# Attention and mixture-of-experts kernel: expert weights issued behind nearly all q, k and V loads, two more of them in the expert stage, scatters of skipped rows issued after their batch's gate

## Chip, cores, metric

The kernel runs on one core of one Trainium2 chip. The metric is device time in microseconds (us) of one execution, all executions judged by state (an execution over 1.5% above the fastest of its kernel counts as slow and is left out of the ratios). "Span" is the profiler's span of one execution; in these runs it is about 1.8 us shorter than the device time of the same execution.

## The reference

```python
# attention: 4 batches, 8 heads, 768 positions, head size 64; 8 global keys, 96 local keys
scores = scale * q @ k.T + bias            # bias: slope of the head times the distance
scores = where(is_global | is_local, scores, -1e9)
x = (softmax(scores) @ v)                  # as rows: x is [3072, 512]
# mixture of experts with early exit: 8 experts, hidden size 1024
do_compute = x @ w_skip > 0                # other rows leave as they are ("skipped rows")
e_idx = argmax(x @ w_gate);  gate_w = softmax(x @ w_gate)[e_idx]
out = x
out[do_compute] = x + gate_w * (relu(x @ w1[e_idx]) @ w2[e_idx])
```

## The kernel before

It works in three stages. Attention goes over 16 units (4 batches of 4 head pairs). The gate of a batch runs within the next batch's units; the last batch's gate stands alone. Then the expert stage: for each expert, gather its rows (two DMAs of 128 rows), multiply, and scatter the result `y` to `out`. Rows that skip the experts are scattered from SBUF, 24 DMAs of 128 rows.

Every load that casts float32 to bfloat16, every gather and every scatter is issued by GpSimd, in program order. One "half" is `w1` or `w2` of one expert: 2 MB read as float32, 1 MB written as bfloat16. There are 16.

```python
    def load_qk(n):                                  # 192 KB each
        nc.gpsimd.dma_start(out=kr[:, :, :], in_=k_r[...])
        nc.gpsimd.dma_start(out=qr[:, :, :], in_=q_r[...])
    def load_half(i, pool):                          # w1 (i even) or w2 (i odd) of expert i // 2
        ...
    EARLY = 5
    wq = list(range(2 * EARLY))                      # ten halves during attention
    halves = {1: 1, 2: 1, 3: 1, 4: 1, 5: 1, 6: 1, 7: 1, 8: 1, 9: 1, 10: 1}
    ...
    for n in range(NU):                              # units
        ...                                          # scores of n + 2, values of n, transposes of n + 4
        if m + 4 < NU:
            load_qk(m + 4)                           # m + 4 = n + 8: q, k of the last units go out at n = 7
        for kind in range(3):
            if extra:
                load_v(vb_, t)                       # 18 V loads, over after n = 5
        for _ in range(halves.get(n, 0)):
            load_half(wq.pop(0), wearly)
        ...                                          # gate and slot placement of batch b - 1
    ...
    def experts(group, first):
        rows, src, gate_ = slot_rows()
        for e in range(E):
            gather(e, src)                           # 2 DMAs
            if first and e % 2 == 1 and EARLY + e // 2 < E:
                load_half(2 * (EARLY + e // 2), wlate)
                load_half(2 * (EARLY + e // 2) + 1, wlate)
        xt = expert_in(0)
        for e in range(E):
            nxt = expert_in(e + 1) if e + 1 < E else None
            expert(e, xt, rows, gate_, group)        # ends in 2 y scatters; y has bufs=4
            if first:
                for t in range(3 * e, 3 * e + 3):
                    skip_out(t, group)               # scatter of skipped rows
            xt = nxt
```

The softmax here doesn't subtract the row's maximum and nothing guards it: scores larger than these inputs give would overflow.

Of the kernel before, what the change touches and what calls it, by code (L numbers as in the profile page):

```python
# [17 lines left out]
def kernel(  # L18
# [13 lines left out]
    nc = tc.nc  # L32
# [3 lines left out]
    T = S // 128  # L36
    N = B * S
    NT = N // 128
    DM = H * D
    HP = H // 2  # L40
    E, F = moe_w1.shape[0], moe_w1.shape[2]
# [13 lines left out]
    EARLY = 5  # L55
# [5 lines left out]
    wearly = ctx.enter_context(tc.tile_pool(name="wearly", bufs=1))  # L61
# [21 lines left out]
    def load_qk(n):  # L83
        b, hp = units[n]
        qr = raw_pool.tile([P, 2, R * D], BF16, tag="qr", name="qr")
        kr = raw_pool.tile([P, 2, R * D], BF16, tag="kr", name="kr")
        nc.gpsimd.dma_start(out=kr[:, :, :], in_=k_r[b, :, 2 * hp:2 * hp + 2, :])
        nc.gpsimd.dma_start(out=qr[:, :, :], in_=q_r[b, :, 2 * hp:2 * hp + 2, :])  # L88
        raws[n] = (qr, kr)
# [6 lines left out]
    def load_v(b, t):  # L96
        nc.gpsimd.dma_start(out=vbs[b][:, t, :, 0:D], in_=v_r[b, t])  # L97
# [3 lines left out]
    def load_half(i, pool):  # L101
        e = i // 2
        if i % 2 == 0:
            w1_sb[e] = pool.tile([128, DC, F], BF16, name=f"w1_{e}")
            nc.gpsimd.dma_start(out=w1_sb[e][:, :, :], in_=w1_r[e])
        else:
            w2_sb[e] = pool.tile([128, FC // 2, 2 * DM], BF16, name=f"w2_{e}")
            nc.gpsimd.dma_start(out=w2_sb[e][:, :, :], in_=w2_r[e])
# [30 lines left out]
    for h in range(H):  # L139
        nc.sync.dma_start(out=vg_f[h * KG:(h + 1) * KG, :, :],  # L140
                          in_=v[:, h, 0:KG, :].rearrange("b k d -> k b d"))
# [27 lines left out]
    for h in range(H):  # L169
        nc.scalar.activation(out=mask8[:, h, :, :],  # L170
                             in_=rel[:, :].unsqueeze(1).to_broadcast([128, 2, W]),
# [57 lines left out]
    skip_k = keep.tile([128, NT], I32)  # L229
# [3 lines left out]
    xbs = [keep.tile([128, T, DM], BF16, name=f"xb{b}") for b in range(B)]  # L233
# [30 lines left out]
    def keys_global(n):  # L264
        b, hp = units[n]
        nc.vector.tensor_tensor(
            out=kg[b % 2][:, hp, 2 * hp * KG:2 * (hp + 1) * KG].rearrange("p (h k) -> p h k", h=2),
            in0=kts[n][:, 0:KG].unsqueeze(1).to_broadcast([128, 2, KG]),
            in1=half_m[:, :].unsqueeze(2).to_broadcast([128, 2, KG]), op=ALU.mult)

    def global_scores(b):
        g_sb = att_pool.tile([128, S], BF16, tag="g_sb", name="g_sb")
        for u in range(2):
            gp = ps_ms.tile([128, R, P // 2], FP32, tag="ms", name="gp")
            for hp in range(HP):
                nc.tensor.matmul(out=gp[:, :, :], lhsT=kg[b % 2][:, hp, :],
                                 rhs=qts[b * HP + hp][:, :, u * (P // 2):(u + 1) * (P // 2)],
                                 start=(hp == 0), stop=(hp == HP - 1))
            nc.scalar.activation(
                out=g_sb[:, u * (S // 2):(u + 1) * (S // 2)].rearrange("a (p r) -> a p r", r=R),  # L280
                in_=gp[:, :, :].rearrange("a r p -> a p r"), func=ACT.Exp, bias=gbias[:, 0:1], scale=scale)
        nc.vector.tensor_tensor(out=g_sb[:, 0:128], in0=g_sb[:, 0:128], in1=m0g[:, :], op=ALU.mult)
        g_sbs[b] = g_sb
# [164 lines left out]
    def place(t0, nt, colid, pool, psum, tag):  # L448
        lo_i = pool.tile([128, nt], I32, tag="lo_i", name="lo_i")
        hi_i = pool.tile([128, nt], I32, tag="hi_i", name="hi_i")  # L450
        nc.vector.tensor_single_scalar(out=lo_i[:, :], in_=s_k[:, t0:t0 + nt], scalar=127,
                                       op=ALU.bitwise_and)
        nc.vector.tensor_single_scalar(out=hi_i[:, :], in_=s_k[:, t0:t0 + nt], scalar=7,
                                       op=ALU.arith_shift_right)
        ohc = pool.tile([128, nt, NCOL], BF16, tag="ohc", name="ohc")
        nc.vector.tensor_tensor(out=ohc[:, :, :],
                                in0=colid[:, :].unsqueeze(1).to_broadcast([128, nt, NCOL]),
                                in1=hi_i[:, :].unsqueeze(2).to_broadcast([128, nt, NCOL]),
                                op=ALU.is_equal)
        bv = pool.tile([128, nt, NV, NCOL], BF16, tag="bv", name="bv")  # L460
        nc.vector.tensor_tensor(
            out=bv[:, :, :, :],
            in0=ohc[:, :, :].unsqueeze(2).to_broadcast([128, nt, NV, NCOL]),
            in1=val_k[:, t0:t0 + nt, :].unsqueeze(3).to_broadcast([128, nt, NV, NCOL]), op=ALU.mult)
        oha = pool.tile([128, nt, 128], BF16, tag="oha", name="oha")
        nc.vector.tensor_tensor(out=oha[:, :, :],
                                in0=row128_i[:, :].unsqueeze(1).to_broadcast([128, nt, 128]),
                                in1=lo_i[:, :].unsqueeze(2).to_broadcast([128, nt, 128]),
                                op=ALU.is_equal)
        sp = psum.tile([128, NV, NCOL], FP32, tag=tag, name="slot_ps")  # L470
        for t in range(nt):
            nc.tensor.matmul(out=sp[:, :, :].rearrange("p a c -> p (a c)"), lhsT=oha[:, t, :],
                             rhs=bv[:, t, :, :].rearrange("p a c -> p (a c)"),
                             start=(t == 0), stop=(t == nt - 1))
        nc.vector.tensor_tensor(out=slots[:, :, :], in0=slots[:, :, :], in1=sp[:, :, :], op=ALU.add)




    extra = [("v", 1, t) for t in range(T)]  # L480
    wq = list(range(2 * EARLY))
    for b in (2, 3):
        extra += [("v", b, t) for t in range(T)]
    halves = {1: 1, 2: 1, 3: 1, 4: 1, 5: 1, 6: 1, 7: 1, 8: 1, 9: 1, 10: 1}
    for n in range(4):
        transposes(n, 1)
        transposes(n, 0)
# [7 lines left out]
    for n in range(NU):  # L495
        b, hp = units[n]
        if hp == 0:
            global_scores(b)
        m, j = n + 4, n + 2
        if j < NU:  # L500
            scores(j, 0)
        values(n, 0)
        if j < NU:
            scores(j, 1)
        if m < NU:
            transposes(m, 1)
            keys_global(m)
        if b > 0 and hp < 3:
            logits(b - 1, hp)
        if j < NU:  # L510
            scores(j, 2)
        values(n, 1)
        if m < NU:
            transposes(m, 0)
        if m + 4 < NU:
            load_qk(m + 4)
        if n in (0, 2, 4):
            make_v(1 + n // 2)
            load_vg(1 + n // 2)
        for kind in range(3):  # L520
            if extra:
                _, vb_, t = extra.pop(0)
                load_v(vb_, t)
        for _ in range(halves.get(n, 0)):
            load_half(wq.pop(0), wearly)
        if hp == HP - 1:
            x_out(b)
        if b > 0 and hp == 2:
            gate(b - 1)
        if b > 0 and hp == 3:  # L530
            gate_rest(b - 1)
            place((b - 1) * T, T, colid_i, gat_pool, ps_ms, "ms")
    for s in range(3):
        logits(B - 1, s, on_vector=(s == 1))
    gate(B - 1)
# [6 lines left out]
    wlate = ctx.enter_context(tc.tile_pool(name="wlate", bufs=1, reuse_waits="tile"))  # L542
# [21 lines left out]
    def gather(e, src):  # L564
        xg[e] = ffn.tile([128, 2, DM], BF16, tag="xg", name="xg", bufs=E)
        for c in range(2):
            nc.gpsimd.indirect_dma_start(  # L567
                out=xg[e][:, c, :], out_offset=None, in_=x_dram[:, :],
                in_offset=bass.IndirectOffsetOnAxis(ap=src[:, 2 * e + c:2 * e + c + 1], axis=0))

    def put(ins, group):
        tc.declare_no_dep(ins.ins, group=group, reason="each row is written once")
        tc.add_to_no_dep_group(group, ins.ins)

    def skip_out(t, group):
        put(nc.gpsimd.indirect_dma_start(  # L576
            out=out[:, :],
            out_offset=bass.IndirectOffsetOnAxis(ap=skip_k[:, t:t + 1], axis=0),
            in_=xbs[t // T][:, t % T, :], in_offset=None, bounds_check=N - 1, oob_is_err=False),
            group)  # L580

    def expert_in(e):
        xp = ps_x.tile([128, DC, CAP], BF16, tag="xp", name="xp")
# [35 lines left out]
    def experts(group, first):  # L619
        rows, src, gate_ = slot_rows()  # L620
        for e in range(E):
            gather(e, src)
            if first and e % 2 == 1 and EARLY + e // 2 < E:
                load_half(2 * (EARLY + e // 2), wlate)
                load_half(2 * (EARLY + e // 2) + 1, wlate)
        xt = expert_in(0)
        for e in range(E):
            nxt = expert_in(e + 1) if e + 1 < E else None
            expert(e, xt, rows, gate_, group)
            if first:  # L630
                for t in range(3 * e, 3 * e + 3):
                    skip_out(t, group)
            xt = nxt

    experts("first", True)
# [58 lines left out]
```

## Time and profile before

| | before |
|---|---|
| device time, median of the runs beside the kernel after | 242.93 us (242.35 to 243.9) |
| span of the profiled run | 242.2 us |
| last attention output | 123.2 us |
| first gather issued | 138.81 us |
| first y scatter issued, landed (after the first gather) | 34.4, 46.1 us |
| TensorE stall on y | 7.68 us |
| last expert matmul ends, end of span (after the first gather) | 80.5, 103.4 us |

Averages over the span say little here, as each stage has its own limit. In the profile PE is TensorE's matmul, PEld its weight load, DVE VectorE, ACT ScalarE and POOL GpSimd. These are the rows of the page that show the stages: one digit per fortieth of the span, about 6 us, in tenths busy; the clock row has the granted TensorE clock, in tenths of full speed.

```profile
PE   1579895995494847768544038699943999992000
DVE  7555896689826236837874611213003332213000
POOL 8776397253443620000000088271716777777710
PEclk9999998897569575559857556999995799998555
DMA  5999999999999999999630039999994355343310
```

The DMA engines are busy throughout attention and idle before the gathers. GpSimd does nothing from 91 to 138 us (eight zeros), while it is the last engine at work, after TensorE, at the end.

**Attention.** Two rows of TensorE's timeline (start, duration, instruction; in brackets the idle time before it and what ended it):

```profile
79.73 0.85 PE L251 MATMUL tr<-ident,kr 96*64 96x96 bf16 x16 [4.26 <-DMA kr<-in_k_dram]
89.22 0.85 PE L251 MATMUL tr<-ident,kr 96*64 96x96 bf16 x16 [3.53 <-DMA kr<-in_k_dram]
```

Units 9 and 10 wait for k. In the trace these two loads were issued at 62.66 and 74.64 and took 17.0 and 14.5 us to land, each right behind a weight half in the queue; the early k loads took about 7.5 us. The windows of the two units (columns: start and end; length; busy time and count of PE, PEld, DVE, ACT, POOL; granted clock; DMA share, which can pass 1 as the tool counts it and is not used here; GB/s) show the price of the wait in the clock as well, 0.62 and 0.68. In the 3.4 us behind each of the two waits it was 0.50:

```profile
76.30:84.60 8.30, 4.87 (x66) 3.75 (x67) 3.60 (x11) 3.01 (x6) 4.03 (x6) 0.62 1.55 192
84.60:94.10 9.50, 5.97 (x100) 4.91 (x98) 3.68 (x10) 4.28 (x6) 1.65 (x3) 0.68 1.15 210
```

**Experts.** GpSimd's timeline: L567 gathers, L105 and L108 weight halves, L614 y scatters, L576 skip scatters.

```profile
152.33 1.01 POOL L567 DMA_INDIRECT xg<-x_rows,src  x1 [0.30 <-issue]
157.31 1.01 POOL L567 DMA_INDIRECT xg<-x_rows,src  x1 [3.97 <-DMA w<-in_moe_w_dram]
...
160.83 0.82 POOL L105 DMA_DIRECT2D w<-in_moe_w_dram  x1
161.62 0.82 POOL L108 DMA_DIRECT2D w<-in_moe_w_dram  x1
164.36 1.02 POOL L567 DMA_INDIRECT xg<-x_rows,src  x1 [1.92 <-DMA w<-in_moe_w_dram]
169.40 1.01 POOL L567 DMA_INDIRECT xg<-x_rows,src  x1 [4.01 <-DMA w<-in_moe_w_dram]
...
173.21 1.03 POOL L614 DMA_INDIRECT out_dram<-y,rows  x1 [0.30 <-DMA xg<-x_rows,src]
174.54 1.00 POOL L614 DMA_INDIRECT out_dram<-y,rows  x1 [0.30 <-issue]
178.20 0.99 POOL L576 DMA_INDIRECT out_dram<-xb,skip_k  x1 [2.65 <-DMA w<-in_moe_w_dram]
183.14 1.00 POOL L576 DMA_INDIRECT out_dram<-xb,skip_k  x1 [3.94 <-DMA w<-in_moe_w_dram]
184.44 0.99 POOL L576 DMA_INDIRECT out_dram<-xb,skip_k  x1 [0.30 <-issue]
...
230.09 1.00 POOL L576 DMA_INDIRECT out_dram<-xb,skip_k  x1 [0.30 <-DMA out_dram<-xb,skip_k]
```

Two readings follow. First, count back eight DMA issues from each one that waited for `w`: it is always the half that had just landed (157.05, 164.10, 169.13, 177.94, 182.87; the waiting issue starts 0.26 to 0.27 us later). So every issue waits for the eighth before it. Second, from 183.14 to the end GpSimd issues one scatter every 1.3 us (1.0 busy, 0.3 between) without a pause.

The y scatter issued at 173.21 landed at 184.95, 2.1 us behind the last half. Until then VectorE had no free y buffer, and TensorE stalled in the middle of expert 3 (VectorE's and TensorE's timelines):

```profile
185.07 1.41 DVE L611 SCALAR_TENSOR_TENSOR y<-yps,gate,xg 128x512 f32<-128x512 f32 x2 [18.55 <-DMA out_dram<-y,rows]
```

```profile
185.87 3.57 PE L606 MATMUL yps<-w,ht 128*128 128x512 bf16 x8 [7.68 <-DVE y L611]
```

### The profile page before, as it was taken

The page shows a single profiled execution, that of the slowest core. Times are in us where ns is not written, and L with a number is a line of the kernel's source. Part 1 is how long each engine was busy: PE and PEld are TensorE (multiplying, and loading weights), DVE is VectorE, ACT ScalarE, POOL GpSimd, SP SyncE. Part 2 cuts the span into 40 slices and gives each one's busy share as a digit, 9 for nine tenths or more (in the row PEclk, how much of TensorE's full clock was granted, in tenths as well). Part 3 has the DMA queues.
Part 4 walks back from the last instruction along what each step waited for, and adds up shares of the span by engine and source line. Part 5 has one row for each costly group of instructions (what it writes and reads, how often), then busy time and mean ns, then how long its engine had stood idle before and what let it go on. Part 6 is the DMA issues. An engine that isn't in the chain of part 4 may idle for free. (4 is left out here: it accounts for less than half of the span.)

```text
span 242.2 us, 4714 instructions
## 1 busy us (share of the span) xinstructions
PE 155.8 (64%) x1877; PEld 110.8 (46%) x1877; DVE 109.1 (45%) x341; ACT 91.8 (38%) x144; POOL 111.0 (46%) x139
## 2 busy tenths in 40 slices
PE   1579895995494847768544038699943999992000
PEld 1455773774353635536544016377621766670000
DVE  7555896689826236837874611213003332213000
ACT  5865983992346433529303002133210222330000
POOL 8776397253443620000000088271716777777710
PEclk9999998897569575559857556999995799998555
DMA  5999999999999999999630039999994355343310
GB/s 79 151 170 194 156 134 189 240 195 185 209 227 209 187 210 209 211 226 237 118 133 0 1 87 177 249 213 237 191 263 132 95 153 153 104 133 110 113 36 0
DMA packets 50521, 38.25 MB, mean 158 GB/s; under 512 B 30276, under 2 KB 39492, under 8 KB 50496
## 3 DMA queue, kind: packets, MB, share of 16 engines
q0 software_dynamic: 45568, 34.62, 85.9%
q1 hardware_dynamic: 4928, 3.30, 5.4%
q8 instruction: 16, 0.26, 0.4%
q14 instruction: 9, 0.07, 0.1%
HBM read 54.68 MB, written 13.63 MB: 282 GB/s over the span
## 5 line engine op out<-in xcount | busy, mean ns | idle before, releaser
L567 POOL DMA_INDIRECT xg<-x_rows,src x16 | 15.7, 980 | 62.2 <-DVE gate L559 48.6
L602 ACT ACTIVATE ht<-hps 128x512 bf16<-128x512 f32 x32 | 19.1, 597 | 65.7 <-PE hps L599 65.7
L315 DVE TENSOR_TENSOR a<-a,mask 128x896 bf16<-128x896 bf16 (+1 forms) x48 | 28.2, 588 | 21.8 <-ACT a L301 11.7
L611 DVE SCALAR_TENSOR_TENSOR y<-yps,gate,xg 128x512 f32<-128x512 f32 x16 | 11.9, 750 | 54.8 <-PE yps L606 33.4
L606 PE MATMUL yps<-w,ht 128*128 128x512 bf16 x128 | 30.8, 395 | 7.7 <-DVE y L611 7.7
L301 ACT ACTIVATE a<-sc 128x896 bf16<-128x896 f32 x32 | 29.0, 923 | 11.2 <-PE sc L296 10.0
L599 PE MATMUL hps<-xt,w 128*128 128x256 bf16 x256 | 31.2, 283 | 0.0
L576 POOL DMA_INDIRECT out_dram<-xb,skip_k x24 | 24.1, 1004 | 13.3 <-DMA w<-in_moe_w_dram 6.6
L599 PEld LDWEIGHTS <-w 128*128 128x128 bf16 x256 | 25.9, 102 | 3.8
L97 POOL DMA_DIRECT2D vb<-in_v_dram x24 | 21.5, 906 | 11.3 <-DMA vb<-in_v_dram 4.0
L606 PEld LDWEIGHTS <-ht 128*128 128x128 bf16 x128 | 12.8, 100 | 22.2 <-issue 9.6
L296 PE MATMUL sc<-qt,kt 64*128 64x224 bf16 x192 | 20.3, 303 | 2.8 <-DVE qt L255 1.3
L333 PE MATMUL av<-vb,a 128*128 128x65 bf16 x192 | 20.7, 215 | 0.0
L251 PE MATMUL tr<-ident,kr 96*64 96x96 bf16 x256 | 11.4, 251 | 13.3 <-DMA kr<-in_k_dram 13.3
L340 PE MATMUL av<-vb,a 128*96 128x65 bf16 x160 | 19.7, 229 | 0.0
L88 POOL DMA_DIRECT2D qr<-in_q_dram x16 | 10.4, 650 | 19.2 <-DMA w<-in_moe_w_dram 11.7
L333 PEld LDWEIGHTS <-a 128*128 128x128 bf16 x192 | 18.6, 125 | 0.0
L346 DVE TENSOR_TENSOR xb<-av,rc 128x384 bf16<-128x384 f32 x32 | 17.8, 558 | 1.1
L614 POOL DMA_INDIRECT out_dram<-y,rows x16 | 15.9, 994 | 4.9 <-issue 3.7
L340 PEld LDWEIGHTS <-a 128*96 128x96 bf16 x160 | 17.1, 147 | 0.0
L251 PEld LDWEIGHTS <-kr 96*64 96x64 bf16 x256 | 8.8, 140 | 17.1 <-DMA kr<-in_k_dram 14.0
L259 ACT ACTIVATE kt<-tr 128x768 bf16<-128x768 bf16 x16 | 13.0, 810 | 8.5 <-PE tr L251 8.5
(117 smaller groups left out, 228.7 us busy)
## 6 DMA issues: line engine op xcount, KB each, us to landing
w<-in_moe_w_dram POOLq DMA_DIRECT2D x16, 1024.0 KB, 17.1
kr<-in_k_dram POOLq DMA_DIRECT2D x16, 192.0 KB, 7.8
qr<-in_q_dram POOLq DMA_DIRECT2D x16, 192.0 KB, 7.9
vb<-in_v_dram POOLq DMA_DIRECT2D x24, 128.0 KB, 10.2
x_rows<-xb SPq DMA_DIRECT2D x4, 768.0 KB, 9.3
out_dram<-xb,skip_k POOLq DMA_INDIRECT x24, 2.6
xg<-x_rows,src POOLq DMA_INDIRECT x16, 12.1
out_dram<-y,rows POOLq DMA_INDIRECT x16, 2.8
```

What stands on the lines that cost most here:

```text
L97: nc.gpsimd.dma_start(out=vbs[b][:, t, :, 0:D], in_=v_r[b, t])
L251: nc.tensor.transpose(out=ps[hh * D:(hh + 1) * D, r, :], in_=raw[:, hh, r * D:(r + 1) * D], identity=ident[0:P, 0:P])
L296: nc.tensor.matmul(out=sc[:, hh, kk, 0:R * wp].rearrange("a (r p) -> a r p", r=R), lhsT=kt[rows, t * 128:(t + 1) * 128], rhs=qt[rows, :, t ...
L301: nc.scalar.activation(out=a[:, :, :].rearrange("a h (k p r) -> a h k p r", k=2, r=R), in_=sc[:, :, :, 0:W].rearrange("a h k (r p) -> a h ...
L315: nc.vector.tensor_tensor(out=a[:, :, 0:wid], in0=a[:, :, 0:wid], in1=m[:, :, 0:wid], op=ALU.mult)
L333: nc.tensor.matmul(out=av[:, jj, hh, :], lhsT=a_sbs[n, t // 2][:, hh, (t % 2) * W:(t % 2) * W + 128], rhs=vb[:, t, h, :], start=False, sto ...
L340: nc.tensor.matmul(out=av[0:NL, jj, hh, :], lhsT=a_sbs[n, p // 2][:, hh, c:c + NL], rhs=vb[:, p, h, :], start=False, stop=(jj == 2 and hh ...
L346: nc.vector.tensor_tensor(out=xb[:, 3 * u:3 * u + 3, 2 * hp * D:(2 * hp + 2) * D].rearrange("p j (h d) -> p j h d", h=2), in0=av[:, :, :, ...
L576: put(nc.gpsimd.indirect_dma_start(out=out[:, :], out_offset=bass.IndirectOffsetOnAxis(ap=skip_k[:, t:t + 1], axis=0), in_=xbs[t // T][:, ...
L599: nc.tensor.matmul(out=hps[:, j, :], lhsT=w1_sb[e][:, dc, c2 * 256 + j:(c2 + 1) * 256:2], rhs=xt[:, dc, :], start=(dc == 0), stop=(dc == D ...
L602: nc.scalar.activation(out=ht[:, c2, :, :], in_=hps[:, :, :], func=ACT.Relu)
L606: nc.tensor.matmul(out=yps[:, :], lhsT=ht[:, f // 2, f % 2, c * 128:(c + 1) * 128], rhs=w2_sb[e][:, f // 2, (f % 2) * DM:(f % 2 + 1) * DM] ...
```

## The change

The intent: keep the weights from delaying q, k and V, and take the skip scatters off GpSimd's busiest stretch by issuing them where GpSimd is idle. It has three parts:

- A: the early halves start in unit 6 instead of unit 1. Unit 6's half still stands ahead of the last q and k loads, those of unit 7.
- B: 18 of the 24 skip scatters are issued before the gathers, two per unit once their batch's gate is done: those of batches 0 and 1 in the units of batches 2 and 3, those of batch 2 behind the last unit. The last batch's six stay with experts 1 to 3.
- C: only eight halves (experts 0 to 3) are loaded early; expert 4's two go into the expert stage, which now has eight halves instead of six.

```diff
-    halves = {1: 1, 2: 1, 3: 1, 4: 1, 5: 1, 6: 1, 7: 1, 8: 1, 9: 1, 10: 1}
+    skips = []
+    halves = {n: 1 for n in range(6, 14)}
 ...  (unit loop)
+        for _ in range(2):
+            if skips:
+                skip_out(skips.pop(0), "first")
         if b > 0 and hp == 3:
             gate_rest(b - 1)
             place((b - 1) * T, T, colid_i, gat_pool, ps_ms, "ms")
+            skips += range((b - 1) * T, b * T)
+    while skips:
+        skip_out(skips.pop(0), "first")
 ...  (experts)
             gather(e, src)
-            if first and e % 2 == 1 and EARLY + e // 2 < E:
-                load_half(2 * (EARLY + e // 2), wlate)
-                load_half(2 * (EARLY + e // 2) + 1, wlate)
+            if first and e % 2 == 1:
+                for i in range(2):
+                    load_half(2 * (E - 4) + e - 1 + i, wearly if e == 1 else wlate)
 ...
             if first:
-                for t in range(3 * e, 3 * e + 3):
-                    skip_out(t, group)
+                if e > 0 and e < 4:
+                    for t in range(NT - T + 2 * e - 2, NT - T + 2 * e):
+                        skip_out(t, group)
```

(The helpers `put` and `skip_out` only move up in the file.)

More of the change, by code (lines that the diff above doesn't have):

```diff
@@ L475, in place, with put, skip_out @@
         nc.vector.tensor_tensor(out=slots[:, :, :], in0=slots[:, :, :], in1=sp[:, :, :], op=ALU.add)
+    def put(ins, group):
+        tc.declare_no_dep(ins.ins, group=group, reason="each row is written once")
+        tc.add_to_no_dep_group(group, ins.ins)
+    def skip_out(t, group):
+        put(nc.gpsimd.indirect_dma_start(
+            out=out[:, :],
+            out_offset=bass.IndirectOffsetOnAxis(ap=skip_k[:, t:t + 1], axis=0),
+            in_=xbs[t // T][:, t % T, :], in_offset=None, bounds_check=N - 1, oob_is_err=False),
+            group)
     extra = [("v", 1, t) for t in range(T)]
     wq = list(range(2 * EARLY))
+    skips = []
     for b in (2, 3):
         extra += [("v", b, t) for t in range(T)]
-    halves = {1: 1, 2: 1, 3: 1, 4: 1, 5: 1, 6: 1, 7: 1, 8: 1, 9: 1, 10: 1}
+    halves = {n: 1 for n in range(6, 14)}
     for n in range(4):
@@ L569, in gather @@
                 in_offset=bass.IndirectOffsetOnAxis(ap=src[:, 2 * e + c:2 * e + c + 1], axis=0))
-    def put(ins, group):
-        tc.declare_no_dep(ins.ins, group=group, reason="each row is written once")
-        tc.add_to_no_dep_group(group, ins.ins)
-    def skip_out(t, group):
-        put(nc.gpsimd.indirect_dma_start(
-            out=out[:, :],
-            out_offset=bass.IndirectOffsetOnAxis(ap=skip_k[:, t:t + 1], axis=0),
-            in_=xbs[t // T][:, t % T, :], in_offset=None, bounds_check=N - 1, oob_is_err=False),
-            group)
     def expert_in(e):
```

## The prediction

> **What bounds the kernel now** (page, windows, timelines): three stages with different limits.
> 1. Attention, to 122.7 us. Units take about 4.2 us at full clock, set by VectorE and TensorE. In units 9 and 10 TensorE waits for a k load: 4.26 us (until 79.73) and 3.53 us (until 89.22). Those loads took 17.0 and 14.5 us to land, because 1 MB weight halves stood before them in the queue; early k loads take about 7.5. A half takes 4.9 to 5.3 us of DMA time.
> 2. Gate of the last batch: first gather at 138.81 us. The DMA row shows 0 here.
> 3. Experts. In GpSimd's timeline every DMA issue waits for the landing of the eighth before it, so six weight halves hold the gathers; the first y scatter issues at 173.21, landing at 184.95, behind the last half (182.87). TensorE stalls 7.68 us on y (four buffers), resumes at 185.87, ends at 219.3. GpSimd issues scatters unbroken, 1.3 us each, until 231; the chain of waits ends there. Last landing 232.7, then 9.5 us to the end, 242.2.
>
> **What the change does.**
> - Halves of experts 0 to 3 move to units 6 to 13, behind nearly all q, k loads: the two k stalls go, and cold clock with them. The Trainium skill, "TensorE: Matmul & The Clock Gate", Part 1, says about 3.4 us of idling halves the clock; this trace agrees (0.50 around both stalls). Units 9 and 10 took 8.3 and 9.5 us; I expect 4.3 each. Gain 8.9 us: first gather at about 130.
> - 18 of 24 skip scatters leave the expert stage: 18 x 1.3 = 23.4 us of GpSimd. They fit into gaps before the gathers. But GpSimd ends only about 11 us after TensorE, so at most 11 can be won.
> - Two more halves (expert 4) enter the expert stage: 2 x 5 = 10 us, in front of the first y scatter. By the eighth-before rule and queue order, expert 0's y lands about 56 us after the first gather instead of 46. TensorE's stall grows from 7.7 to about 18, and its end moves from 80.5 to about 91 us after the first gather. The Trainium skill, "DMA: Bandwidth & Descriptors", "Issuing engines are not separate DMA queues", says all DMAs share 16 engines; the trace agrees (that scatter lands 2.1 us after the last half).
>
> So the expert stage ends with TensorE, not GpSimd: last landing about 94.5, end about 104 us after the first gather; today 103.4. What freeing GpSimd gains, the longer y stall eats.
>
> **Sum.** 243.1 - 8.9 (k stalls, clock) - 11 (backlog) + 10.5 (y stall) + 0.5 = 234.2; I say 234.5 us, range 230.5 to 239. Chances: faster by over 2% 0.84, within 2% 0.14, slower 0.02.
>
> **What would show it.** No TensorE wait on k loads after the start; first gather near 130; DMA busy until about 100 us, idle before the gathers; VectorE's wait for y's scatter about 28 us, TensorE stalled about 18 within expert 3; no back-to-back scatters at the end, TensorE's last matmul within 4 us of the last landing.
>
> **What would make it wrong.** The y stall not growing (scatters overtaking weights, or halves faster than 5 us): about 225. The attention gain lost to other waits, or the clock at half after the gates: about 240. GpSimd, blocked on skip rows, holding a weight half so long that it meets the gathers: slower.

## The result, and the profile after

| | before | after |
|---|---|---|
| device time, median | 242.93 us | 235.87 us (235.46 to 236.07) |
| ratio, 95% interval | | 0.9703 (0.9669 to 0.9738) |
| span of the profiled run | 242.2 | 234.0 |
| units 9 and 10 | 8.3, 9.5 | 4.1, 4.2 |
| first gather issued | 138.81 | 129.33 |
| first y scatter issued, landed (after the first gather) | 34.4, 46.1 | 40.4, 58.2 |
| TensorE stall on y | 7.68 | 19.54 |
| last expert matmul ends, end of span (after the first gather) | 80.5, 103.4 | 91.7, 104.7 |

Times in us. A ratio is the mean time of one kernel's fast runs over that of the kernel before's fast runs of the same rounds, so it is not quite the ratio of the medians quoted.

The same rows of the page, after:

```profile
PE   1569995985769757695451179699800079999700
DVE  7554996498845888478838021130000061232300
POOL 8765596666572232641360775633436057333210
PEclk9999997699758985598575559999965569999975
DMA  5999999999999999999960299999999633311110
```

GpSimd now works through attention and thins out at the end. But TensorE has a hole of three slices (zeros), 170 to 187 us, in the middle of the expert stage; before, a smaller one stood there.

Units 9 and 10 in windows, to be set against the two of before: half as long, and the clock is 1.00.

```profile
76.40:80.50 4.10, 3.59 (x80) 2.83 (x79) 3.43 (x10) 3.96 (x7) 0.93 (x2) 1.00 1.12 210
80.50:84.70 4.20, 2.90 (x75) 2.41 (x69) 3.47 (x11) 2.99 (x5) 0.99 (x1) 1.00 1.19 238
```

GpSimd's timeline in the expert stage (L585 gathers, L621 y scatters, L482 skip scatters):

```profile
164.75 0.82 POOL L105 DMA_DIRECT2D w<-in_moe_w_dram  x1
165.54 0.84 POOL L108 DMA_DIRECT2D w<-in_moe_w_dram  x1
169.73 1.04 POOL L621 DMA_INDIRECT out_dram<-y,rows  x1 [3.35 <-DMA w<-in_moe_w_dram]
174.65 1.02 POOL L621 DMA_INDIRECT out_dram<-y,rows  x1 [3.87 <-DMA xg<-x_rows,src]
...
220.33 0.97 POOL L621 DMA_INDIRECT out_dram<-y,rows  x1 [4.25 <-DVE y L618]
222.06 0.97 POOL L621 DMA_INDIRECT out_dram<-y,rows  x1 [0.76 <-DVE cnt_i L650]
```

Expert 7's two halves now stand right ahead of the first y scatter, in the program and in the queue. At the end GpSimd waits for VectorE's y instead of running a backlog. VectorE and TensorE in the middle:

```profile
187.66 1.41 DVE L618 SCALAR_TENSOR_TENSOR y<-yps,gate,xg 128x512 f32<-128x512 f32 x2 [30.41 <-DMA out_dram<-y,rows]
```

```profile
188.47 3.40 PE L613 MATMUL yps<-w,ht 128*128 128x512 bf16 x8 [19.54 <-DVE y L618]
```

So the whole gain, 8.2 us of span, is in attention (the first gather comes 9.5 us earlier); the expert stage became 1.3 us longer although 18 scatters left it.

### The profile page after: what moved, and what is told of

It reads as the page before. It is cut to its first block, busy times and chain, and to the rows that moved or that the text cites. A ratio compares the mean times of both kernels' runs of the same rounds, so it can differ in the third digit from the quotient of the medians.

```text
span 234.0 us, 4720 instructions
## 1 busy us (share of the span) xinstructions
PE 150.0 (64%) x1877; PEld 106.2 (45%) x1877; DVE 108.5 (46%) x341; ACT 91.3 (39%) x144; POOL 112.1 (48%) x139
## 4 chain that ended last, share of the span: by engine, by line
DMA 30%; PE 25%; DVE 20%; ACT 9%; issue 6%; POOL 5%; POOLq 0%; ACTq 0%; DVEq 0%
DMA out_dram<-y,rows 8%; DMA w<-in_moe_w_dram 8%; PE yps L613 7%; DMA kr<-in_k_dram 6%; PE hps L606 6%; DMA xg<-x_rows,src 5%; DVE xb L346 4%; DVE a L315 4%; DMA qr<-in_q_dram 4%; PE gp L276 3%; ACT xts L376 3%; ACT a L301 3%; ACT a L309 3%; POOL xg L585 2%; DVE qt L255 2%
## 5 line engine op out<-in xcount | busy, mean ns | idle before, releaser
L613 PE MATMUL yps<-w,ht 128*128 128x512 bf16 x128 | 30.6, 393 | 19.5 <-DVE y L618 19.5
L618 DVE SCALAR_TENSOR_TENSOR y<-yps,gate,xg 128x512 f32<-128x512 f32 x16 | 11.9, 750 | 65.8 <-PE yps L613 34.4
L482 POOL DMA_INDIRECT out_dram<-xb,skip_k x24 | 25.0, 1042 | 35.1 <-DMA w<-in_moe_w_dram 17.9
L621 POOL DMA_INDIRECT out_dram<-y,rows x16 | 15.7, 981 | 33.2 <-DVE y L618 23.4
L585 POOL DMA_INDIRECT xg<-x_rows,src x16 | 15.6, 976 | 22.0 <-DMA w<-in_moe_w_dram 11.6
L296 PE MATMUL sc<-qt,kt 64*128 64x224 bf16 x192 | 19.6, 293 | 3.1 <-ACT a L301 1.3
L333 PE MATMUL av<-vb,a 128*128 128x65 bf16 x192 | 19.3, 208 | 0.0
L340 PE MATMUL av<-vb,a 128*96 128x65 bf16 x160 | 18.5, 220 | 0.0
L333 PEld LDWEIGHTS <-a 128*128 128x128 bf16 x192 | 17.2, 118 | 0.0
L340 PEld LDWEIGHTS <-a 128*96 128x96 bf16 x160 | 15.8, 139 | 0.0
L376 ACT ACTIVATE xts<-xt_ps 128x1024 bf16<-128x1024 bf16 x11 | 11.3, 1030 | 10.0 <-PE xt_ps L369 9.7
L251 PE MATMUL tr<-ident,kr 96*64 96x96 bf16 x256 | 10.9, 243 | 6.5 <-DMA kr<-in_k_dram 6.5
```

What stands on the lines that cost most here:

```text
L296: nc.tensor.matmul(out=sc[:, hh, kk, 0:R * wp].rearrange("a (r p) -> a r p", r=R), lhsT=kt[rows, t * 128:(t + 1) * 128], rhs=qt[rows, :, t ...
L333: nc.tensor.matmul(out=av[:, jj, hh, :], lhsT=a_sbs[n, t // 2][:, hh, (t % 2) * W:(t % 2) * W + 128], rhs=vb[:, t, h, :], start=False, sto ...
L340: nc.tensor.matmul(out=av[0:NL, jj, hh, :], lhsT=a_sbs[n, p // 2][:, hh, c:c + NL], rhs=vb[:, p, h, :], start=False, stop=(jj == 2 and hh ...
L482: put(nc.gpsimd.indirect_dma_start(out=out[:, :], out_offset=bass.IndirectOffsetOnAxis(ap=skip_k[:, t:t + 1], axis=0), in_=xbs[t // T][:, ...
L585: nc.gpsimd.indirect_dma_start(out=xg[e][:, c, :], out_offset=None, in_=x_dram[:, :], in_offset=bass.IndirectOffsetOnAxis(ap=src[:, 2 * e ...
L613: nc.tensor.matmul(out=yps[:, :], lhsT=ht[:, f // 2, f % 2, c * 128:(c + 1) * 128], rhs=w2_sb[e][:, f // 2, (f % 2) * DM:(f % 2 + 1) * DM] ...
```

## The experiments

All outputs are right. The kernel before was timed beside each call's kernels: 243.44, 243.57 and 243.4 us (median). First the three parts, in combinations.

### a_only: the order of the early halves alone

```diff
 kernel before
-    halves = {1: 1, ..., 10: 1}
+    halves = {n: 1 for n in range(6, 16)}
```

> Kernel before, with only the order of the ten early weight halves changed: one each in units 6 to 15 instead of 1 to 10. Skip scatters stay in the expert stage, six halves stay there. My ledger: no TensorE wait on k loads after the start, units 9 and 10 at 4.2 us each, first gather at 129.5 us instead of 138.8, expert stage unchanged at 103.4 us after it; about 234 us, ratio 0.963. Rival 1 (the k stalls went because fewer halves lie in the attention stage, not because of their order): with ten halves a wait on q, k or on the x rows comes back, first gather later than 132. Rival 2 (most of the change's gain comes from the scatters): under 1% faster.

Measured: 235.02 us, ratio 0.9632 (0.9576 to 0.9688). TensorE does not wait for k after the start; units 9 and 10 take 4.1 and 4.2 us; first gather at 130.5 us; end 103.9 us after it; stall on y 7.9 us. The same ten halves in a later order give the whole attention gain, so rival 1 falls: it is order, not amount. Rival 2 falls too.

### b_only: the skip scatters alone

The edit is the change's skip-scatter part on the kernel before, without the two weight hunks.

> Kernel before, with only the skip scatters moved as in the change; weights as before. My ledger: first gather stays near 138.8; TensorE stall on y stays about 7.7 us and its last matmul near 80.5 us after the first gather; the backlog of GpSimd after TensorE's end goes, so the last landing is about 85 and the end about 94.7 us after the first gather: about 234.3 us, ratio 0.964. Rival (the scatters' backlog was hidden, or moves the gathers or k loads when spread over attention): within 1% of before, or first gather later than 140.

Measured: 232.66 us, ratio 0.9546 (0.9494 to 0.9598): this third of the change alone is faster than all of it. First gather at 139.8 us; the k waits are still there (4.53 and 3.49 us); stall on y 7.6 us; last matmul 80.5 and end 93.4 us after the first gather. GpSimd's last rows in its timeline wait for VectorE, as intended:

```profile
219.64 0.97 POOL L621 DMA_INDIRECT out_dram<-y,rows  x1 [4.25 <-DVE y L618]
221.36 0.97 POOL L621 DMA_INDIRECT out_dram<-y,rows  x1 [0.75 <-DVE cnt_i L650]
```

### ab: both, with expert 4's halves still early

```diff
 kernel after
-    halves = {n: 1 for n in range(6, 14)}
+    halves = {n: 1 for n in range(6, 16)}
 ...  (experts: weights of experts 5, 6, 7 only, as in the kernel before)
```

> Kernel after, but expert 4's two halves loaded in units 14 and 15, as in a_only, so that six halves lie in the expert stage. My ledger, in which the extra two halves cost 10 us of TensorE stall on y: first gather 129.5, y stall about 8 us instead of 19.5, end about 94.7 us after the first gather: about 225 us, ratio 0.926. Rival (the two halves cost nothing there, as the DMA engines have slack after them): 235 to 236 us as the kernel after. In doubt: the last halves may run into the gathers (10 halves end near 127 us), which would add 1 to 4 us.

Measured: 223.53 us, ratio 0.9188 (0.9119 to 0.9258). First gather at 128.7 us, although the last early half landed only at 128.4; stall on y 7.5 us; end 92.5 us after the first gather. A saves 3.7% and B 4.5%; both together save 8.1%, so they add up. Against the kernel after (0.9698 in its repetition below), part C costs about 0.051 of 243.5 us, 12.4 us; the intervals of the two ratios leave about 2.4 us either way, and the traces' time from first gather to end, 104.7 and 105.0 against 92.5 us, agrees.

### ac: weights as in the change, skip scatters as before

The edit is the change's two weight hunks on the kernel before.

> Kernel after, but the 24 skip scatters back in the expert stage, three behind each expert's y scatters. My ledger: first gather 129.5; first y scatter issued near 40 us after it, second near 45, then 38 more scatters at 1.3 us, the last issued near 95 and landed near 97, end near 107 us after the first gather: about 237 us, ratio 0.976. So with expert 4's halves in the expert stage moving the scatters is worth only about 2 us. Rival (moving 18 scatters is worth 11 us, or 23, whatever else is done): 247 us or more.

Measured: 242.01 us, ratio 0.9939 (0.989 to 0.9988; one slow run is left out of the ratio). The size was missed by 5 us. The first profiled execution had a span of 237.2 us and the others 239.1 to 240.9, so a second trace was taken.

> ac once more for a second trace: its profiled execution had a span of 237.2 us where the others had 239.1 to 240.9. If that execution only had faster weight loads, this one's second y scatter issues near 45.4 us after the first gather (42.7 there) and its span is 239 to 241 us. If it again has 42.7 with a longer span, the difference is elsewhere.

Measured: one run, state unknown, span 240.9 us. The second y scatter was issued 45.5 us after the first gather, as expected (42.7 in the first trace, where the halves landed earlier). GpSimd's timeline of this second trace shows what my sum had left out:

```profile
174.29 1.03 POOL L614 DMA_INDIRECT out_dram<-y,rows  x1 [3.92 <-DMA w<-in_moe_w_dram]
...
182.13 0.99 POOL L614 DMA_INDIRECT out_dram<-y,rows  x1 [1.61 <-DMA w<-in_moe_w_dram]
186.54 1.00 POOL L576 DMA_INDIRECT out_dram<-xb,skip_k  x1 [3.42 <-DMA w<-in_moe_w_dram]
...
228.17 0.99 POOL L576 DMA_INDIRECT out_dram<-xb,skip_k  x1 [0.31 <-DMA out_dram<-y,rows]
```

I had counted 38 scatters at 1.3 us from 174 on; but two of them again wait for the eighth issue before, which are expert 7's halves: 1.61 + 3.42 us. The backlog then runs to 228.2 us. So A and C without B gain only 0.6%: the 9 us of attention come back as backlog. B is worth about 6 us on top of A and C, not 2 as I expected, and 11 us alone.

### after_again: the kernel after as control

> The kernel after, unchanged, as the control on the same chip: ratio 0.970 to the kernel before, about 236 us; TensorE stall on y 16 to 20 us inside expert 3, the first y scatter lands 55 to 58 us after the first gather.

Measured: 235.7 us, ratio 0.9698 (0.9629 to 0.9767); stall on y 19.9 us; first y scatter landed 58.7 us after the first gather.

### late_w7: same bytes, other order

```diff
 kernel after
-            if first and e % 2 == 1:
+            if first and e % 2 == 1 and e < 7:
 ...
             expert(e, xt, rows, gate_, group)
+            if first and e == 1:
+                load_half(2 * (E - 1), wlate)
+                load_half(2 * (E - 1) + 1, wlate)
```

> Kernel after, but expert 7's two halves issued behind the y scatters of experts 0 and 1 instead of ahead of them. Same bytes in the same stage, same y buffers; only the queue order differs. If the queue order of y's scatter behind the last halves makes the stall (my ledger): first y scatter issued about 34 and landed about 46 us after the first gather, y stall 7 to 8 us, end 93 to 95 us after the first gather, about 224 us, as ab. Rival (the amount of weight traffic in the expert stage makes it, whatever the order): y stall stays over 15 us, 234 to 237 us. Expert 7's weights must land before about 70 us after the first gather, I expect 56.

Measured: 224.06 us, ratio 0.9204 (0.9149 to 0.9259). First y scatter issued 35.2 and landed 45.6 us after the first gather; end 93.1 us after it. In TensorE's timeline the stall is back at its old size:

```profile
175.36 3.57 PE L613 MATMUL yps<-w,ht 128*128 128x512 bf16 x8 [7.04 <-DVE y L618]
```

The expert stage still loads eight halves, and the time is ab's within 0.6 us. So part C's cost is not the traffic but the place of the first y scatter behind expert 7's halves. The rival falls.

### y7: the wait made harmless instead

```diff
 kernel after
-            y = ffn.tile([128, DM], FP32, tag="y", name="y", bufs=4)
+            y = ffn.tile([128, DM], FP32, tag="y", name="y", bufs=7)
```

> Kernel after with seven y buffers instead of four (the most that fits). The scatters wait as before: first y scatter lands 55 to 58 us after the first gather. If the delayed scatter costs time only through the four buffers: TensorE runs three more output groups before it stalls, the stall starts near 52 us after the first gather and lasts 3 to 8 us, last matmul near 78, end 90 to 93 us after the first gather, about 223 us. Rival (TensorE is held up by the late weights themselves and the y wait only covers it): stall of the same total, moved to weight loads or gathers, 234 to 237 us.

Measured: 227.75 us, ratio 0.9354 (0.9282 to 0.9426); end 97.2 us after the first gather. The second y scatter landed 59.1 us after the first gather, as late as in the kernel after (58.4), so the buffers alone take 8 us off. (Builds with 8, 10 and 16 buffers did not fit in SBUF.) My size was missed by 5 us, and TensorE's and VectorE's timelines say why:

```profile
188.74 5.96 PE L606 MATMUL hps<-xt,w 128*128 128x256 bf16 x32 [11.52 <-DVE xt L597]
```

```profile
187.34 0.75 DVE L618 SCALAR_TENSOR_TENSOR y<-yps,gate,xg 128x512 f32<-128x512 f32 x1 [18.89 <-DMA out_dram<-y,rows]
188.00 0.68 DVE L597 COPY xt<-xp 128x512 int32<-128x512 int32 x1
```

I had counted free buffers in PSUM, the memory that matmuls write to. But here VectorE took its work in program order: standing before a y without a buffer, it also held back the copy of expert 5's input. TensorE had written that input by 177.2 us; the copy started at 188.00, right behind the y, and TensorE stalled 11.5 us for it.

### c10: two more halves ahead of y

```diff
 kernel after
-    halves = {n: 1 for n in range(6, 14)}
+    halves = {n: 1 for n in range(6, 12)}
 ...  (experts)
-                for i in range(2):
+                for i in range(-2 if e == 1 else 0, 2):
```

> Kernel after with expert 3's two halves moved into the expert stage as well (issued with expert 4's, ahead of the third gather): ten halves there, eight of them... all ten ahead of the first y scatter. If each half ahead of y delays it by its 5 us of queue time: first y scatter lands about 68 us after the first gather (46 with six, 58 with eight), y stall about 29 us, last matmul near 102, end about 115 us after the first gather, about 246 us, slower than the kernel before. One doubt: the third gather now lands 10 us later too, so part of the stall may stand before expert 2 instead; the end should be the same. Rival (the cost of the first two halves was a threshold, the next two are free): 235 to 238 us.

Measured: 242.8 us, ratio 0.9965 (0.9891 to 1.004): 7 us slower than the kernel after, not 10. First y scatter landed 65.4 us after the first gather. The stall stands in two places in TensorE's timeline, together 27.9 us:

```profile
156.01 1.03 PE L593 MATMUL xp<-ident,xg 128*128 128x128 bf16 x8 [11.98 <-DMA xg<-x_rows,src]
...
193.87 3.57 PE L613 MATMUL yps<-w,ht 128*128 128x512 bf16 x8 [15.91 <-DVE y L618]
```

No threshold, then: further halves ahead of y cost time again. With four, six, eight and ten halves ahead of it (ab_late below, ab, after, c10) the first y scatter landed 34.7, 46.0, 58.2 and 65.4 us after the first gather. The last step is 7 and not 10 us, and the trace says where the rest went: the two added halves landed 4.94 and 5.00 us behind the half ahead of each, but the later stretches, in which four gathers and a pair of halves follow each other, became shorter by 1.3, 1.0 and 0.5 us. Why they became shorter stays open. (This run, like ac_again, was made on another chip than the others; its ratio is against the kernel before on that chip.)

### ab_late: the version that the experiments point to

It is ab with late_w7's move: four halves ahead of the first y scatter, expert 7's two behind those of experts 0 and 1.

> ab with the same move: four halves ahead of the first y scatter, expert 7's two behind those of experts 0 and 1. First y scatter lands about 34 us after the first gather, before TensorE needs it at 39.4; no TensorE stall on y over 1 us; last matmul at 71 to 73 and end at 84 to 86 us after the first gather: about 215.5 us, ratio 0.885. Rival (the stall is set by something else than the halves ahead of y): 222 to 225 us as ab.

Measured: 214.4 us, ratio 0.8846 (0.878 to 0.8912). The first y scatter landed 34.7 us after the first gather, and TensorE's timeline has no wait on y; last matmul 70.3 and end 83.3 us after the first gather. This beats both kernels.

| kernel | parts | device time, us | ratio | first gather | stall on y | gather to end |
|---|---|---|---|---|---|---|
| a_only | A | 235.02 | 0.9632 | 130.5 | 7.9 | 103.9 |
| b_only | B | 232.66 | 0.9546 | 139.8 | 7.6 | 93.4 |
| ab | A, B | 223.53 | 0.9188 | 128.7 | 7.5 | 92.5 |
| ac (ac_again's trace) | A, C | 242.01 | 0.9939 | 128.7 | 19.4 | 112.2 |
| after_again | A, B, C | 235.7 | 0.9698 | 129.1 | 19.9 | 105.0 |
| late_w7 | A, B, C reordered | 224.06 | 0.9204 | 128.9 | 7.0 | 93.1 |
| ab_late | A, B, six halves reordered | 214.4 | 0.8846 | 128.5 | none | 83.3 |

## Why the prediction was right

- **The k waits are due to the halves ahead in the queue, and moving the halves removes them.** Right, shown by a_only. Predicted gain 8.9 us; a_only's ratio gives 0.0368 x 243.4 = 9.0 us. The first gather was predicted at about 130 and came at 129.33. The clock behaved as "TensorE: Matmul & The Clock Gate", Part 1, of the Trainium skill says of idle windows of about 3.4 us, which bring it to half: 0.50 in the 3.4 us behind each wait, so 0.62 and 0.68 over units 9 and 10; 1.00 without the waits. How the 9 us divide between waiting (4.26 + 3.53 us) and a slower clock was not tried separately.
- **Of the 23.4 us of issue time that leave GpSimd's last stretch, at most 11 can be won.** Right, shown by b_only: 0.0454 x 243.4 = 11.1 us. After that TensorE ends the stage.
- **Two more halves ahead of y lengthen the stall on y, and this eats the second gain.** Right in mechanism, shown by late_w7, which undoes the loss by order alone. The size was a little small: 10.5 us predicted, about 12.4 measured (ab against after_again). The mis-sized term is the landing of the first y scatter, 58.2 us after the first gather instead of 56. The prediction counted two halves at 5 us. In the trace of after, four gathers also stand between the sixth half (landed at 173.84) and the seventh (181.88). These two are 8.04 us apart, as are the halves at the other two such places in that trace (8.43 and 7.96), against 4.9 to 5.0 within a pair.
- **The sum.** 243.1 - 8.9 - 11 + 10.5 + 0.5 = 234.2, stated as 234.5; measured 235.87, inside the range. (The prediction does not say where its 0.5 comes from.) Each of the three terms came out close by itself, so the hit is not owed to errors that cancel. The measured terms, -9.0 - 11.1 + 12.4 = -7.7 us, fit the measured 7.1 to 7.4.
- **The signs.** No k wait after the start (only 1.04 us at 17.4); VectorE's wait 30.4 us (28 predicted); TensorE stalled 19.5 (18) inside expert 3; last matmul 3.6 us before the last landing (within 4). One sign was wrong: DMA was to be idle from about 100 us; the last early half landed at 117.4. GpSimd was not what was late: it issued that half at 96.46, when the half ahead of it was still 14.8 us from landing, so the half waited in the queue. The early halves landed 6.3 us apart on average, not 5. The trace shows one thing that shares the time: a half that landed 7.6 us behind the one ahead of it, at 106.37, did so while a store of the attention rows was under way (92.7 to 107.3). Being late cost nothing, as the first gather came at 129.3 (ab even had a half land at 128.4 and kept its first gather).
- **A citation that this trace does not test.** The prediction cites the skill for DMAs of all issuers sharing the same 16 engines and takes as agreement that the y scatter landed 2.1 us behind the last half. Both are issued by GpSimd, so this shows only their order. Sharing between issuers shows elsewhere in the trace of before: three early halves that were under way together with a store issued by SyncE (102.0 to 115.9) landed 5.3, 6.7 and 5.6 us behind the half ahead of each, against 4.9 to 5.2 us in the three pairs of the expert stage.

## What to carry to other kernels

Where, as here, nearly all DMAs go through one in-order issuer and one queue, a small store can land as late as the last load put ahead of it (2.1 us behind it in the kernel before; 12.6 us earlier after the first gather in late_w7 than in after, by order alone): put loads that are needed late behind the stores that free buffers early. Work moved off a busy engine is worth only the time by which that engine outlasts the next one (11 of 23.4 us in b_only), so find that next limit first. The Trainium skill, "Perfetto Trace Analysis", Optimization Strategy, says that kernels with several regimes can gain by interleaving them; b_only, which moves scatters from the expert stage into attention, agrees (4.5%), and ac, which moves weight loads about without that, gains almost nothing (0.6%).

## What the Trainium skill lacked or had wrong

- "DMA: Bandwidth & Descriptors", Issuing engines are not separate DMA queues, calls the issue time "usually small relative to the DMA itself". Scatters of 128 rows from GpSimd are an exception to that "usually": one issue per 1.3 us against a median of 2.6 to 2.8 us to landing on the page of the kernel before, and the unbroken run from 183 to 231 us set the end of the kernel before.
- The same page, Anatomy of one DMA, gives 2.0 us plus bytes over 436,000 per us and does not say which bytes count when a load casts. Here a half that reads 2,097,152 B as float32 and writes 1 MB landed 4.9 to 5.2 us after the half ahead of it, in the three pairs of the kernel before's expert stage. An estimate with that page's rate gives 4.8 us for the bytes read and 2.4 for the bytes written, so the bytes read fit, as far as one size can tell.
- No page has the wait for the eighth DMA issue before (five of five waits on weights in the expert stage of the kernel before, each ended 0.26 to 0.27 us after that landing). The traces also show what waits: GpSimd's 128 DMAs post their landing to eight semaphores in turn, and in the kernel before 100 of the 120 issues behind the first eight carry, or follow, an instruction that waits for the semaphore they will use. So the wait is written in the program as built; whether the hardware would need it is not shown.
- No page says what mixing gathers with large loads in one queue costs. In the kernel before, four gathers of 128 rows landed within 1.0 us behind the last half, and within 1.1 and 3.6 us where two more halves followed them; in the kernel after the last four took 2.7 us. What sets this spread is not shown.
